# First product of the first strip: seven products of half size in place of eight for the last two groups of W_in

## The chip, the cores and the metric

The kernel runs on one core of one Trainium2 chip. The metric is the device time of one execution in microseconds; the number given for a kernel is the median of its runs. Next to the runs there is one profiled execution, whose trace and page are read here. Engines are PE (TensorE; PEld is its weight loading), DVE (VectorE), ACT (ScalarE), POOL (GpSimd) and SP, whose queue issues the DMAs.

## The reference

```
kv  = einsum('bhsd,bhse->bhde', k, v)              # 8 batches, 8 heads, 576 tokens, 64 features
o   = einsum('bhsd,bhde->bhse', q, kv)
x   = o / sqrt(mean(o*o) + 1e-6) * g_norm          # per token and head
x   -> 4608 tokens x 512
h   = x @ w_in                                     # 512 x 2048
out = max(h, 0)**2 @ w_out                         # 2048 x 512
```

All of it is done in fp32. W_in and W_out come as 64-bit floats and are taken apart into fp32 on the chip.

## The kernel before

**Strips.** The 4608 tokens are taken in nine strips of 512. Each strip has a first product (x times W_in, then ReLU and square into the tiles `gt`) and a second product (times W_out, then out). The attention of later batches is cut into small slices that `attend` puts between the steps of the products. Everything is issued in the order in which the program is written: `manual_schedule` leaves that order alone, and each engine works through its own queue in that order.

**Seven products.** From the second strip on, both products are made by the scheme of Strassen and Winograd: operands are cut in halves both ways, and seven products of the halves, of sums and of differences take the place of eight (the second strip's second product, and both products of later strips, apply the scheme twice). `ORDER = (1, 2, 6, 5, 7, 3, 4)` is their order. Products 1, 6, 7 and 4 add up in PSUM bank A, 5 and 3 in bank B, and 2 is alone in bank C. After products 1, 6 and 5, ACT copies the bank into a `snap` tile (pool "c", six buffers); after 2, 7 and 3, VectorE adds a snap to the bank and so makes a quarter of the result; product 4 leaves the last quarter in bank A (`combine`, line 875). For the first product (`up`, line 920) VectorE then makes ReLU and square of each quarter (lines 933 and 934), except the last, which ACT makes (938 and 939). The operands are the blocks 0 to 3 of W_in (`w_in`, of which block 1 is overwritten by block 0 minus block 1), its sums s1, s2, s4 in blocks 4 to 6 (`w_s`), and x with four differences (`sums_x`).

**The first strip.** Its second product is already made by seven products (`down`). Its first product is not: it runs over four groups of W_in's columns (`NG`), each group over two halves `fh` and two blocks `i`, 16 steps of `up_first` (line 903). A step is one PSUM tile of 128 x 512 with four matmuls over the inner dimension (each matmul leaves two records in the trace), a ReLU on ACT (line 916) and two squares on ACT into the quarters (line 918). The tile steps may run ahead of ACT by four PSUM buffers.

**The weights' conversion, in between.** After each step i of `up_first`, `convert(PACE[i])` converts pieces of W_in and then of W_out, a pair of pieces at a time (16 pairs; pairs 0 to 7 are W_in, two a group; 8 to 11 are the first half of W_out, 12 to 15 the second). For a pair ACT makes two passes (lines 260 and 262, `w_c` and `raw`), always one pair ahead; GpSimd clamps `w_c` (line 282); VectorE joins the words in two operations (lines 284 and 288). For pairs 12 to 15 `sums_out` adds four VectorE sums of W_out's blocks, which SP then stores to `w_out` in DRAM; the second product streams them back as `w_blk`. In the places of W_in's sums, `w_s`, lie the first three blocks of W_out until the first strip is done with them; so W_in's own sums are made only during the second product (`sums_in`, line 314: ACT scales the four blocks by g, VectorE makes four sums a group).

**Around it.** The steps of the attention of batch 1 (transposes of queries `t_ps`, called T below, and key-value products `kv_ps`, called K) stand after the last six steps of the first product. At the second product's start VectorE makes the sums of `gt` (`g_s`), then the sums of W_out's quarters for later strips (`w_t`, sent to `w_deep`), then W_in's sums, then the differences of the second strip's x.

Of the kernel before, what the change touches and what calls it, by code (L numbers as in the profile page):

```python
# [10 lines left out]
FP32 = mybir.dt.float32  # L11
# [3 lines left out]
AF = mybir.ActivationFunctionType  # L15
ALU = mybir.AluOpType
# [4 lines left out]
def kernel(  # L21
# [54 lines left out]
    SQ = 32  # L76
    Q_ON_PE = 2
    BEHIND = 1.6
    X_ON_PE = 2
    EPS = 1e-6  # L80
    AHEAD = 10
# [228 lines left out]
    def pieces_in(i):  # L310
        g, k = divmod(i // 2, KH)
        convert_pair(i // 2, w_in[:, k, g].rearrange("p (a b) e -> p a (b e)", a=2))

    def sums_in(g):

        nc.scalar.activation(w_in[:, :, g, 0:4], w_in[:, :, g, 0:4], AF.Copy, scale=g_col)
        a11, a21, a12, a22, s1, s2, s4 = (block(b)[:, :, g] for b in range(7))
        nc.vector.tensor_tensor(out=s1, in0=a21, in1=a22, op=ALU.add)
        minus(nc.vector, s2, s1, a11)
        minus(nc.vector, s4, a12, s2)  # L320
        minus(nc.vector, a21, a11, a21)
# [24 lines left out]
    def convert(n):  # L346
        while converted[0] < min(n, len(conversions)):
            fn, a = conversions[converted[0]]
            fn(a)
            converted[0] += 1  # L350
# [340 lines left out]
        return xt[s][:, ts(th, TH // SQ), ts(kh, KH), :]  # L691

    def sums_x(s):
        xc[s] = t1, t2, t3, t4 = [
            sum_pool.tile([P, TH // SQ, KH, SQ], FP32, name=f"x_t{i}", tag="sum") for i in range(4)
        ]
        x = lambda kh, th: halves(s, kh, th)
        minus(nc.vector, t1, x(0, 1), x(0, 0))
        minus(nc.vector, t2, x(1, 1), t1)
        minus(nc.vector, t3, x(1, 1), x(0, 1))  # L700
        minus(nc.vector, t4, x(1, 0), t2)
# [165 lines left out]
    def product(p, i, lhsT, rhs, n):  # L867

        for k in range(n):
            nc.tensor.matmul(  # L870
                bank[BANK[p]][:, i, :], lhsT=lhsT(k), rhs=rhs(k),
                start=p in (1, 5, 2) and i == 0 and k == 0, stop=k == n - 1, skip_group_check=True,
            )
# [13 lines left out]
    def quarters(s, g):  # L887

        if (s, 11) not in gq:
            for q in (11, 12, 21, 22):  # L890
                gq[s, q] = g_pool.tile([P, FQ, TH], FP32, name="gt", tag="gt")
        return {q: gq[s, q][:, 2 * g : 2 * g + 2, :] for q in (11, 12, 21, 22)}
# [27 lines left out]
    def up(s, g, p):  # L920
        open_bank(p)
        rhs = {
            1: halves(s, 0, 0), 2: halves(s, 1, 0), 3: halves(s, 1, 1),
            4: xc[s][3], 5: xc[s][0], 6: xc[s][1], 7: xc[s][2],
        }[p]
        for i in range(2):
            product(p, i, lambda kc: block(A_IN[p])[:, kc, g, ts(i, P)], lambda kc: rhs[:, :, kc, :], KH)
        dest = quarters(s, g)

        def relu_squared(q):  # L930
            def f(b, a):
                o = dest[q]
                nc.vector.tensor_tensor(out=o, in0=b, in1=a, op=ALU.add)
                nc.vector.scalar_tensor_tensor(out=o, in0=o, scalar=0.0, in1=o, op0=ALU.max, op1=ALU.mult)
            return f

        def last(b):
            nc.scalar.activation(dest[21], b, AF.Relu)
            nc.scalar.activation(dest[21], dest[21], AF.Square)

        combine(p, relu_squared(11), relu_squared(12), last, relu_squared(22))
# [417 lines left out]
    for s in range(N_STRIP):  # L1359
# [7 lines left out]
        if s >= DEEP_UP:  # L1367
            steps = [(0.5, up_slot, (s, slot)) for slot in range(55)]
        elif s == 0:
            steps = [(2, up_first, (g, fh, i)) for g in range(NG) for fh in range(2) for i in range(2)]  # L1370
        else:
            steps = [(1, up, (s, g, p)) for g in range(NG) for p in ORDER]
        n_up = len(steps)
# [6 lines left out]
        if s >= DEEP_UP:  # L1380
            goal = max(goal, min(ready[DEEP_UP] + (len(slices) - ready[DEEP_UP]) * (s - 1) // (N_STRIP - DEEP_UP - 1), len(slices)))
            if s > DEEP_UP:
                goal = min(pair_ends, key=lambda end: abs(end - goal))
        total, done = sum(w for w, _, _ in steps), 0
        for i, (w, fn, a) in enumerate(steps):
            if s == 0 and i < n_up:

                if i == 0:
                    load_next()
                    load_rest(1, nc.sync)  # L1390
                    load_next()
                if i == 1:
                    load_next()
                if i == 2:
                    for b in range(2):
                        load_q_rest(b, nc.sync)
                if i == 14:
                    for b in range(2):
                        store_first(b)
            elif s == 0 and i == n_up:  # L1400
                convert(len(conversions))
                conv.close()

                stream_pool = ctx.enter_context(tc.tile_pool(name="stream", bufs=6, reuse_waits="tile"))
                sum_pool = ctx.enter_context(tc.tile_pool(name="sum", bufs=8, reuse_waits="tile"))
            if s == 0 and n_up <= i < n_up + 2:
                for g in range(2 * (i - n_up), 2 * (i - n_up) + 2):
                    sum_g1(0, g)
            if s == 0 and n_up + 2 <= i < n_up + 4:
                for g in range(2 * (i - n_up) - 4, 2 * (i - n_up) - 2):  # L1410
                    sum_g3(0, g)
            fn(*a)
            if s == 0 and i < n_up:

                convert(PACE[i])
            done += w
            if s:
                clock[0] += 3.2 if i >= n_up else 2.2 if s == DEEP else 1.2
                soon = tiles_due and tiles_due[0][2][0] // NT == s + 1
                if i == n_up + 10:  # L1420
                    while tiles_due and tiles_due[0][2][0] // NT == s + 1:
                        _, f, a = tiles_due.popleft()
                        f(*a)
                elif not due(keys_due) and not (soon and due(tiles_due)):
                    least = 2.1 if s == DEEP else 4.5 if i < n_up else 3.3
                    quiet = n_up * 2 // 3 < i < n_up + 3 or s == DEEP and (i > n_up + 9 or i == n_up + 7)
                    quiet = quiet or s == DEEP and i < n_up and drips and drips[0][0] == load_q_rest
                    if not quiet and clock[0] >= dripped[0] + least:
                        dripped[0] = clock[0]
                        drip(True)  # L1430
                        if s == DEEP and i == n_up + 8:
                            drip(True)
                if s == DEEP:
                    attend(begun + (goal - begun) * min(i + 1, 25) // 25)
                elif i < n_up:
                    attend_between(i, begun, goal, *(2, 34) if s == DEEP_UP else (0, 27), 38)
                if s == DEEP and i in (3, 4, 7, 9):
                    if i == 3:
                        last_sums = store_deep_sums(*deep_due.popleft())
                    next(last_sums, None)  # L1440
                if s == DEEP and i == n_up - 3:
                    leaf_sums(s, 4)
                if s == 1 and i in range(2, 23, 3):
                    deep_sums_in((1, 6, 5, 4, 0, 2, 3)[i // 3])
                if s == 1 and i in (17, 20, 21, 23):
                    stream()
                continue
            if i == n_up:
                nc.gpsimd.memset(open_xt(1)[:, 0, 0, 0:1], 0.0)
                stream(2)  # L1450
            if i == n_up + 4:
                stream()
            if i in (n_up + 8, n_up + 11):
                load(2, (i - n_up) // 11, nc.sync, "q")
            if i == n_up + 12:
                load_q_rest(2, nc.sync)
            if i - n_up in (7, 8, 9, 12):
                sums_in((7, 8, 9, 12).index(i - n_up))
            if i == n_up + 11:
                sums_x(1)  # L1460
            n = i + 1 - (n_up - 6)
            pairs, m = divmod(max(n - 2 * NP, 0), 3)
            attend(min(ready[0] + min(max(n, 0), 2 * NP) + (n >= 2 * NP) + 4 * pairs + (0, 2, 2)[m], goal))
            while deep_due and i not in (n_up + 1, n_up + 4, n_up + 12, n_up + 13):
                deque(store_deep_sums(*deep_due.popleft()), 0)
            if i == n_up + 2:
                store_first(2)
            if i == n_up + 3:
                for _ in range(2):
                    load_next(names="kv")  # L1470
            if i == n_up + 6:
                load_rest(2, nc.sync)
# [30 lines left out]
```

## Time and profile before

| | |
|---|---|
| median of 3 runs | 870.62 us (869.41 to 871.22) |
| the profiled execution | 868.8 us, span 867.0 us |
| PE, PEld busy | 857.8 us (99%), 804.2 us (93%) |
| VectorE busy | 702.0 us (81%) |
| ACT, GpSimd busy | 348.9 us (40%), 328.1 us (38%) |
| first product of the first strip on PE | to 82.3 us from the span's start |
| second product of the first strip on PE | 83.06 to 138.2 us |

The span runs from the first to the last instruction. A row of the timeline gives start, duration, engine, line, operation, out<-in, shapes and how many instructions were merged; in brackets stands the engine's idle time before it and what ended that. Rows of the busy times by stretch give from:to, length, then each engine's busy time with the number of instructions.

### The profile page before, as it was taken

To read this page: it belongs to the slowest core of one execution; us is meant where nothing else is said; L and a number is where in the kernel's file an instruction comes from. 1 tells how busy PE (TensorE), PEld (TensorE's weight loads), DVE (VectorE), ACT (ScalarE), POOL (GpSimd) and SP (SyncE) were. 2 spreads that over 40 slices of the span, in tenths; PEclk is the share of its full clock that TensorE was granted. 3 is DMA by queue.
4 is the path that set the end of the run, shared out by engine and by line. 5 is a ranking of instruction groups with operands and counts; after the bars stand their busy time and mean duration, and the time that the engine had idled before them with its cause. 6 is when DMAs were issued, how large, how long until landed. Compare 5 with 4: busy or idle time off the path is not lost.

```text
span 867.0 us, 32426 instructions
## 1 busy us (share of the span) xinstructions
PE 857.8 (99%) x14176; PEld 804.2 (93%) x14176; DVE 702.0 (81%) x1132; ACT 348.9 (40%) x777; POOL 328.1 (38%) x335
## 2 busy tenths in 40 slices
PE   7999999999999999999999999999999999999998
PEld 6445888889999999999999999999999999999998
DVE  3768988879877996789688967897889777975887
ACT  4888241320048303750356034901491148102810
POOL 1223004630458223730574045704470447145700
PEclk9999999999999999999999999999999999999999
DMA  9898998999999997989698979987678856885583
GB/s 307 277 362 269 274 377 239 295 332 353 280 264 259 342 325 233 228 307 344 209 244 273 341 239 281 283 297 270 198 236 302 301 165 221 293 282 196 175 315 121
DMA packets 169469, 236.46 MB, mean 273 GB/s; under 512 B 78704, under 2 KB 133744, under 8 KB 161008
## 3 DMA queue, kind: packets, MB, share of 16 engines
q1 hardware_dynamic: 169024, 234.33, 83.5%
q8 instruction: 111, 1.82, 0.9%
q14 instruction: 30, 0.25, 0.1%
q10 hardware_dynamic: 304, 0.07, 0.0%
HBM read 197.66 MB, written 36.70 MB: 270 GB/s over the span
## 4 chain that ended last, share of the span: by engine, by line
PE 83%; DMA 7%; DVE 5%; ACT 3%; SPq 1%; issue 1%; DVEq 0%; ACTq 0%
PE ps_A L865 36%; PE ps_B L865 31%; PE ps_C L865 5%; PE ps_A L870 4%; DMA raw<-in_moe_w_in_dram 2%; PE kv_ps L448 2%; PE x_ps L484 2%; PE ps_B L870 2%; DVE w_t L306 1%; DMA w_deep<-w_t 1%; DMA raw<-in_moe_w_out_dram 1%; DMA w_blk<-w_deep 1%; PE ps_C L870 1%; DMA first_qkv<-in_v_dram 1%; ACT w_c L260 1%
## 5 line engine op out<-in xcount | busy, mean ns | idle before, releaser
L865 PE MATMUL ps_B<-w_blk,g_s 128*64 128x128 f32 x2016 | 122.0, 273 | 0.0
L865 PEld LDWEIGHTS ps_B<-w_blk,g_s 128*64 128x64 f32 x2016 | 112.6, 137 | 0.1
L306 POOL TENSOR_TENSOR x_l<-xT 128x256 f32<-128x256 f32 x21 | 16.2, 773 | 230.2 <-PE ps_A L865 230.2
L865 PE MATMUL ps_B<-w_blk,gt 128*64 128x128 f32 x1504 | 94.1, 273 | 0.3 <-DMA w_blk<-w_deep 0.3
L865 PE MATMUL ps_A<-w_blk,g_s 128*64 128x128 f32 x1536 | 92.2, 273 | 0.0
L1323 POOL TENSOR_TENSOR snap<-snap,gt 128x512 f32<-128x512 f32 x35 | 46.2, 1320 | 112.5 <-ACT snap L1328 93.6
L865 PEld LDWEIGHTS ps_A<-w_blk,g_s 128*64 128x64 f32 x1536 | 85.7, 137 | 0.0
L865 PEld LDWEIGHTS ps_B<-w_blk,gt 128*64 128x64 f32 x1504 | 84.6, 137 | 0.8 <-PE ps_B L865 0.5
L1328 ACT COPY snap<-ps_A 128x512 f32<-128x512 f32 x63 | 36.8, 585 | 103.6 <-PE ps_A L865 96.2
L1263 ACT ACTIVATE gt<-gt 128x512 f32<-128x512 f32 x112 | 70.2, 627 | 9.9 <-DVE gt L1323 9.9
L1264 ACT ACTIVATE gt<-gt 128x512 f32<-128x512 f32 x112 | 70.7, 631 | 3.5
L865 PE MATMUL ps_A<-w_blk,gt 128*64 128x128 f32 x1152 | 71.2, 273 | 0.0
L865 PEld LDWEIGHTS ps_A<-w_blk,gt 128*64 128x64 f32 x1152 | 64.7, 137 | 0.0
L1112 ACT COPY o_sb<-ps_A 128x128 f32<-128x128 f32 x24 | 6.4, 265 | 144.7 <-PE ps_A L865 109.4
L306 DVE TENSOR_TENSOR gt<-gt 128x2048 f32<-128x2048 f32 (+1 forms) x29 | 59.7, 2063 | 0.0
L1111 DVE TENSOR_TENSOR o_sb<-o_sb,ps_B 128x256 f32<-128x256 f32 (+1 forms) x123 | 47.4, 386 | 14.3 <-ACT o_sb L1112 9.5
L865 PE MATMUL ps_A<-x_l,w_in 128*64 128x128 f32 x896 | 58.6, 273 | 0.2 <-DVE gt L1323 0.2
L1323 POOL TENSOR_TENSOR gt<-gt,snap 128x512 f32<-128x512 f32 x42 | 52.5, 1279 | 15.1 <-DVE snap L1323 15.1
L865 PEld LDWEIGHTS ps_A<-x_l,w_in 128*64 128x64 f32 x896 | 50.8, 137 | 0.5 <-DVE gt L1323 0.5
L865 PE MATMUL ps_B<-x_l,w_blk 128*64 128x128 f32 x784 | 51.2, 273 | 0.0
L865 PE MATMUL ps_A<-x_l,w_blk 128*64 128x128 f32 x784 | 51.2, 273 | 0.0
L1112 ACT COPY o_sb<-ps_B 128x128 f32<-128x128 f32 x31 | 8.2, 265 | 96.3 <-PE ps_B L865 96.3
(214 smaller groups left out, 1900.2 us busy)
## 6 DMA issues: line engine op xcount, KB each, us to landing
w_blk<-w_deep SPq DMA_DIRECT2D x56, 1024.0 KB, 7.3
w_blk<-w_out SPq DMA_DIRECT2D x56, 768.0 KB, 6.2
w_blk<-w_in_deep SPq DMA_DIRECT2D x49, 768.0 KB, 5.8
raw<-in_moe_w_in_dram SPq DMA_DIRECT2D x16, 512.0 KB, 9.2
raw<-in_moe_w_out_dram SPq DMA_DIRECT2D x16, 512.0 KB, 8.0
k<-in_k_dram SPq DMA_DIRECT2D x29, 256.0 KB, 4.9
v<-in_v_dram SPq DMA_DIRECT2D x29, 256.0 KB, 5.2
x_d<-x_q SPq DMA_DIRECT2D x27, 256.0 KB, 4.8
```

Of the source, the lines that this page charges most:

```text
L260: nc.scalar.activation(c, high_f, AF.Copy, scale=EXPONENT)
L306: eng.tensor_tensor(out=out, in0=a, in1=b, op=ALU.subtract)
L448: nc.tensor.matmul(ps[ts(h, D), i], lhsT=a, rhs=w, start=i == 0 and c == 0, stop=c == C, skip_group_check=True)
L484: nc.tensor.matmul(ps[half, r, i, ts(p, D)], lhsT=q[row, half], rhs=kvd[b, p][row, row], start=True, stop=True)
L865: nc.tensor.matmul(ps[half], lhsT=lhsT[:, half], rhs=rhs, start=start, stop=stop, skip_group_check=True)
L870: nc.tensor.matmul(bank[BANK[p]][:, i, :], lhsT=lhsT(k), rhs=rhs(k), start=p in (1, 5, 2) and i == 0 and k == 0, stop=k == n - 1, skip_gro ...
L1111: add = lambda out, a, b: nc.vector.tensor_tensor(out=out, in0=a, in1=b, op=ALU.add)
L1112: yield nc.scalar.copy(q[:, 3:4], small(1))
L1263: nc.scalar.activation(o, o, AF.Relu)
L1264: nc.scalar.activation(o, o, AF.Square)
L1323: add = lambda eng, out, a, b: eng.tensor_tensor(out=out, in0=a, in1=b, op=ALU.add)
L1328: nc.scalar.copy(t, ps)
```

## The change

Groups 2 and 3 of the first strip's first product are made by `up`, the seven products, in place of four steps of `up_first` each; groups 0 and 1 stay (`PLAIN = 2`). The first product then has 8 + 14 steps; the counter `at` maps them onto the 16 places at which loads, conversions and attention slices were put before.

The seven products need operands that did not exist at that point:
- the four differences of the first strip's x, made by VectorE after step 5, in four of the six buffers of pool "c";
- W_in's sums for groups 2 and 3, made by VectorE (`first_sums_in`, before the conversion at step 6 and after step 11). As `w_s` holds W_out, they lie in the quarters 22, 12 and 21 of these groups' activations, each of which is written only after its sum was read. Block 1 is overwritten by its difference at once, so that `sums_in` later makes s2 and s1 from the difference, with three VectorE operations in place of four.

Of the results, VectorE makes three additions a group and two ReLU-squares; ACT makes ReLU and square of the quarters 12 and 21 and the three snaps.

```diff
+    PLAIN = 2
...
+    first_w = {}
+
+    def first_sums_in(g):
+
+        a11, a21, a12, a22 = (block(b)[:, :, g] for b in range(4))
+        dest = quarters(0, g)
+        s1, s2, s4 = first_w[g] = [dest[q] for q in (22, 12, 21)]
+        nc.vector.tensor_tensor(out=s1, in0=a21, in1=a22, op=ALU.add)
+        minus(nc.vector, s2, s1, a11)
+        minus(nc.vector, s4, a12, s2)
+        minus(nc.vector, a21, a11, a21)
+
     def sums_in(g):
 
         nc.scalar.activation(w_in[:, :, g, 0:4], w_in[:, :, g, 0:4], AF.Copy, scale=g_col)
         a11, a21, a12, a22, s1, s2, s4 = (block(b)[:, :, g] for b in range(7))
+        if g >= PLAIN:
+            minus(nc.vector, s2, a22, a21)
+            nc.vector.tensor_tensor(out=s1, in0=s2, in1=a11, op=ALU.add)
+            minus(nc.vector, s4, a12, s2)
+            return
...
     def sums_x(s):
+        pool, tag = (sum_pool, "sum") if s else (c_pool, "c")
         xc[s] = t1, t2, t3, t4 = [
-            sum_pool.tile([P, TH // SQ, KH, SQ], FP32, name=f"x_t{i}", tag="sum") for i in range(4)
+            pool.tile([P, TH // SQ, KH, SQ], FP32, name=f"x_t{i}", tag=tag) for i in range(4)
         ]
...
         for i in range(2):
-            product(p, i, lambda kc: block(A_IN[p])[:, kc, g, ts(i, P)], lambda kc: rhs[:, :, kc, :], KH)
+            b = A_IN[p]
+            w = first_w[g][b - 4] if s == 0 and b > 3 else block(b)[:, :, g]
+            product(p, i, lambda kc: w[:, kc, ts(i, P)], lambda kc: rhs[:, :, kc, :], KH)
...
                 nc.vector.tensor_tensor(out=o, in0=b, in1=a, op=ALU.add)
+                if s == 0 and q == 12:
+                    nc.scalar.activation(o, o, AF.Relu)
+                    nc.scalar.activation(o, o, AF.Square)
+                    return
                 nc.vector.scalar_tensor_tensor(out=o, in0=o, scalar=0.0, in1=o, op0=ALU.max, op1=ALU.mult)
...
-            steps = [(2, up_first, (g, fh, i)) for g in range(NG) for fh in range(2) for i in range(2)]
+            steps = [(2, up_first, (g, fh, i)) for g in range(PLAIN) for fh in range(2) for i in range(2)]
+            steps += [(1, up, (s, g, p)) for g in range(PLAIN, NG) for p in ORDER]
...
-        total, done = sum(w for w, _, _ in steps), 0
+        total, done, at = sum(w for w, _, _ in steps), 0, -1
+        plain, turns = 4 * PLAIN, 4 * NG
         for i, (w, fn, a) in enumerate(steps):
-            if s == 0 and i < n_up:
+            if s == 0:
+                before, at = at, i if i < plain else plain + (i - plain) * (turns - plain) // (n_up - plain)
+                if i >= n_up:
+                    at = turns + i - n_up
+            if s == 0 and at < turns and at > before:
...
-                if i == 14:
+                if at == 14:
                     for b in range(2):
                         store_first(b)
...
             fn(*a)
             if s == 0 and i < n_up:
 
-                convert(PACE[i])
+                if i == plain - 3:
+                    sums_x(0)
+                if i == plain - 2:
+                    first_sums_in(PLAIN)
+                if at > before:
+                    convert(PACE[at])
+                if i == plain + 3:
+                    first_sums_in(PLAIN + 1)
...
-            n = i + 1 - (n_up - 6)
+            n = at + 1 - (turns - 6)
```

## The prediction

> **What bounds the kernel now.** I read the granted clock first (1.000 throughout), then busy time by stretch, then the chain that ended last, then the timeline of VectorE and GpSimd. The change lies between 46 us, where the second group's weights are converted, and 131 us, where the first strip's second product is in its last term. In the busy times by stretch (length, then PE, PEld, DVE, ACT, POOL, granted clock, DMA share, GB/s):
>
> ```profile
> 46.00:58.00 12.00, 12.00 (x30) 5.30 (x29) 7.25 (x7) 9.52 (x16) 3.30 (x3) 1.00 1.10 328
> 58.00:70.00 12.00, 11.78 (x49) 5.29 (x47) 7.51 (x7) 11.90 (x19) 4.96 (x4) 1.00 0.96 370
> 70.00:83.00 13.00, 12.93 (x72) 6.51 (x72) 12.70 (x13) 12.80 (x26) 4.06 (x5) 1.00 0.77 229
> 83.00:92.70 9.70, 9.70 (x127) 8.35 (x122) 9.49 (x13) 2.97 (x10) 0.00 (x0) 1.00 1.08 308
> 92.70:131.20 38.50, 38.08 (x244) 33.06 (x243) 35.20 (x62) 13.74 (x17) 0.00 (x0) 1.00 0.98 333
> ```
>
> PE is full, so the page looks like a TensorE bound. But from 70 us VectorE is full too, and the chain that ended last runs on it from 81 to 131 us (apart from one transfer of 10.4 us at 105 us), until PE waits for it:
>
> ```profile
> 81.05 0.68 DVE wt L306
> 81.73 1.99 DVE w_c L284
> ...
> 130.58 0.61 DVE o_sb L1042
> 131.24 8.90 PE ps_A L870 x40
> ```
>
> PE and VectorE are level at 131.24: PE idles 0.46 us there for the o_sb addition, which reads the bank that p=4 adds into. After that PE idles 0.03 us up to 195, so what is lost by 131 is lost for good.
>
> The last thing to see is that VectorE and GpSimd do not run side by side on SBUF data. Timeline rows (start, duration, engine):
>
> ```profile
> 81.39 1.24 POOL L282 TENSOR_SCALAR w_c<-w_c 128x1024 f32<-128x1024 f32 x1 [2.14 <-ACT w_c L260]
> 81.64 2.06 DVE L284 SCALAR_TENSOR_TENSOR w_c<-w_c,raw 128x1024 int32<-128x1024 int32 x1
> 83.74 1.23 DVE L288 SCALAR_TENSOR_TENSOR wt<-raw,w_c 128x1024 int32<-128x1024 int32 x1
> ...
> 27.85 1.05 POOL L282 TENSOR_SCALAR w_c<-w_c 128x1024 f32<-128x1024 f32 x1 [2.25 <-DVE newton L515]
> 28.11 0.69 DVE L605 TENSOR_TENSOR x_n<-x_ps,newton 128x512 f32<-128x512 f32 x1
> ```
>
> The 2.06 is a 1.23 operation that began under a clamp of GpSimd and ended 1.07 us after it. The 28.11 row, which reads PSUM, runs inside a clamp at its usual 0.69.
>
> **What PE gains.** A tile of 512 tokens takes 3.44 us (starts 51.08, 54.51, 57.95), a group of four 13.75. One of the seven products takes 1.73 us in the second strip (138.25 to 139.98), seven 12.1. Two groups save 3.3 us.
>
> **What VectorE gets, all before 131 us.** Prices are distances from start to start.
> - Differences of x: the same four take 136.89 to 139.42, 2.53 us.
> - Sums of W_in: four a group, 122.66 to 125.32, so 2 x 2.66 = 5.32.
> - Combinations: addition and ReLU-square 1.32 (163.02 to 164.34), twice a group, and one bare addition 0.60; 3.24 a group, 6.48.
>
> Together 14.3 us. Nothing is taken from VectorE before 131: the two operations saved in sums_in (0.7 us each) are those of groups 2 and 3, which start at 131.10 and 139.42, where PE waits for no one, so they bring nothing.
>
> **Room for it.** VectorE's gaps from 46.06 (end of pair 5) to 92.66 (end of the last sums of W_out) are 1.41, 0.93, 2.31, 1.68, 0.93, 0.93 and 0.93 = 9.1 us. In each of the seven a clamp of about 0.93 runs, which VectorE's SBUF operations can't share; 2.6 us are free. The six additions read PSUM and may lie beside a clamp, 3.6 us. So 14.3 - 2.6 - 3.6 = 8.1 us late at 92.7. From there to 130.5 there are waits of 0.55, 0.28 and 1.67 us. The first two are for ACT and go away; the third is for w_deep's transfer, which starts from VectorE's own w_t and moves with it: I give it half. VectorE arrives 8.1 - 0.8 - 0.8 = 6.5 us late, between 5.6 (all absorbed) and 8.1.
>
> **PE meets the same delay earlier.** PE's fourth product of the last group (p=4) needs the addition of p=7, which stands on VectorE behind pair 13. Adding up the order that the code issues from 46.06, with a converted pair 2.49, its clamp 0.93 and its four sums 2.54: differences 2.5; pair 6 with clamp 3.4; sums of group 2 2.7; pairs 7, 8, 9 with clamps 10.3; p=2's addition and square 1.3 (clamp beside); pair 10 2.5; sums of group 3 2.7; p=7's 1.3 (clamp beside); pair 11 2.5; p=3's addition 0.6, its clamp standing out by 0.3; pair 12 with sums 5.0; p=2's 1.3; pair 13 with sums 5.0. That is 41.4, so 87.5 us. The addition (0.7), p=4 (1.73) and K (0.74) follow: the second product starts at 90.7 instead of 83.06, 7.6 us late. From there PE is full to 130.78, so it would reach the last term at 138.4, against VectorE's 137.6 (131.1 + 6.5). Small waits between dependent operations (0.2 each where a square stands behind a clamp, four times) put it 0.8 later, at 139.2. Against 131.24 that is 7.2 to 8.0: the idle 0.46 goes first. I take **+7.6 us**, the middle, since both engines come out there; ends 5.6 (VectorE with every wait absorbed, PE no later than it) and 11.2 (the six additions not beside clamps, 3.6 more).
>
> **The rest, at no cost.** ACT loses 8 tiles x 1.17 = 9.4 us and gets six snaps at about 0.5 and eight passes at about 0.55, 7.4: 2 us less. ACT is full from 58 to 83, but VectorE's queue covers it. What is new is that a snap waits for PE and, as xc[0] holds four of the six "c" buffers, for the addition that frees the fifth or sixth; behind it stand the next pair's passes (one pair ahead of need) and the copies of T and K. If that lead is used up, VectorE idles (rival 2). PE gets waits for snaps after p=1, 6, 5, each with one product (1.73) of lead, while ACT has been starting its tiles up to 1.7 us after PE's end (57.95 to 59.61); T and K stand behind, and they are late with everything else. GpSimd's queue holds only clamps, which come later with VectorE. SP: the raw pieces wait for VectorE's last pass five pairs before, with 8 to 10 us of landing against over 17 us of lead; w_out's stores, the key and value loads (issued 78.24, used 90.61) and w_blk move with the work that releases them.
>
> **Rivals.**
> 1. *It is hidden, faster by PE's 3.3: 867.3.* For it: VectorE is busy 81% of the span and its gaps are 9.1 us. Against: all room to 131, clamps' share excluded, is 2.6 + 3.6 + 2.5 = 8.7. It decides where VectorE's load fits before 130.5, that is 14.3 + 3.3 us of room.
> 2. *Lockstep: +12.6, 883.2.* The additions find no clamp to lie beside (3.6), and the waits for snaps and "c" buffers use up ACT's lead once or twice (a late pair's passes are 2.1 us on ACT, of which 1.4 is left after the four 0.2s above). For it: ACT is 99% busy at 58 to 70.
> 3. *Clamps don't block: +4.4, 875.* The whole 9.1 us is room: 14.3 - 9.1 - 0.8. Against: the 2.06 row.
> 4. *The clock falls in a stall.* By the order above PE waits about 5 us for the snap of p=1 behind pair 9's passes, more than any wait of before (1.4). At the trace's start, after idling, 14 records of 128x128 take 3.22 us, 0.23 each, and four at 7.17 take 0.71, 0.18 each; 14 then lose 0.7 to 1.4 us. After the first stall this hides behind PE's later waits; only if one comes before the last products it adds all of that, +9.0: 879.6. [...]
>
> **Numbers.** The profiled execution took 868.8 us (span 867.0 and 1.8 around it), 1.8 below the median of the runs, 870.62; a fixed shift adds to either, and I give the median: 870.6 + 7.6 = 878.2. Chances: forecast 0.72 (876 to 882), rival 2 0.10, rival 4 0.05, rival 3 0.06, rival 1 0.07. From 873 to 885 all but rival 1 and the tails is held. A measurement can tell 0.2% (1.7 us) from no change; faster 0.06, same 0.02, slower 0.92.
>
> **What would show it.** Right: VectorE without real gaps from 46 to about 100 us; the last w_s sums near 100; the second product near 91; PE idle about 11 us more in all between 52 and 91, in waits for snaps and for gt additions; from there the same rows 7 to 9 us later, PEclk 1.00. Wrong: VectorE gaps not filled by clamps, additions stretched by clamps, or PE starting its second product at 80.

## The result, and the profile after

The changed kernel takes 882.25 us (median of 4 runs, 881.97 to 885.62) against 870.85 us for the kernel before (median of 4, 869.41 to 871.22). The ratio of the means is 1.0143, 95% interval 1.0116 to 1.017. By the medians it is slower by 11.4 us. Its profiled execution took 882.1 us, with a span of 880.2 us and a mean granted clock of 0.994; the one of before took 868.8 us, with a span of 867.0 us at 1.000.

Busy times by stretch of the changed kernel; the columns are from:to, length, PE, PEld, DVE, ACT, POOL (each with its instructions), granted clock, DMA share, GB/s:

```profile
46.00:58.00 12.00, 7.82 (x27) 4.66 (x25) 11.86 (x12) 8.59 (x15) 3.22 (x3) 1.00 1.09 317
58.00:70.00 12.00, 9.71 (x34) 8.12 (x35) 10.86 (x11) 9.39 (x11) 4.64 (x4) 0.72 0.94 365
70.00:83.00 13.00, 8.99 (x58) 7.07 (x57) 12.79 (x15) 6.65 (x12) 1.59 (x2) 0.99 0.27 89
83.00:92.70 9.70, 9.70 (x57) 7.98 (x57) 8.97 (x11) 6.14 (x9) 2.68 (x3) 0.83 0.95 282
92.70:131.20 38.50, 38.50 (x340) 33.38 (x339) 35.09 (x60) 13.43 (x25) 0.00 (x0) 1.00 0.99 321
```

PE, which was full in each of these stretches, is now idle for 4.2, 2.3 and 4.0 us in the first three. VectorE is full from 46 us on instead of from 70, but for one wait of 0.93 us. The granted clock, 1.00 everywhere before, is 0.72 and 0.83 in two stretches. The PE timeline of the changed kernel (start, duration, operation; in brackets the idle time and what ended it) shows the three waits:

```profile
51.92 1.89 PE L889 MATMUL ps_C<-xT,w_in 128*128 128x256 f32 x8
60.29 3.78 PE L889 MATMUL ps_A<-x_t,gt 128*128 128x256 f32 x8 [6.48 <-ACT snap L899]
63.87 2.84 PE L889 MATMUL ps_B<-x_t,gt 128*128 128x256 f32 x8
...
72.24 1.99 PE L889 MATMUL ps_A<-x_t,w_in 128*128 128x256 f32 x8 [1.65 <-DVE gt L954]
...
81.42 2.43 PE L889 MATMUL ps_A<-x_t,gt 128*128 128x256 f32 x8 [2.36 <-ACT snap L899]
...
93.90 3.72 PE L889 MATMUL ps_A<-w_s,gt 128*128 128x256 f32 x16
```

The first and the third wait are for ACT's snap after product 1 of group 2 and of group 3; the one between is for the addition of product 7. The last row is the second product's start: 93.90 instead of 83.06. The products right behind the two snaps last 3.78 and 2.43 us where the usual row is 1.89: that is the lower clock, 0.50 from 60.20 to 63.70 and 0.80 from 81.40 to 83.80. ACT's timeline shows what held the first snap:

```profile
53.67 1.15 ACT L261 ACTIVATE w_c<-raw 128x1024 f32<-128x1024 f32 x1 [2.75 <-DMA raw<-in_moe_w_out_dram]
...
57.59 1.15 ACT L261 ACTIVATE w_c<-raw 128x1024 f32<-128x1024 f32 x1 [0.56 <-DMA raw<-in_moe_w_out_dram]
...
59.66 0.58 ACT L899 COPY snap<-ps_A 128x512 f32<-128x512 f32 x1
...
75.94 0.63 ACT L956 ACTIVATE gt<-gt 128x512 f32<-128x512 f32 x1 [5.11 <-DVE gt L954]
...
80.78 0.59 ACT L899 COPY snap<-ps_A 128x512 f32<-128x512 f32 x1
```

The snap of product 1, which PE had finished near 52, stands behind the passes of two pairs of W_out whose raw pieces land only at 53.6 and 57.5. That is not VectorE's doing: in the kernel before the same pass of pair 9 begins at 57.53, behind the same transfer. The second one, at 80.78, stands behind ACT's ReLU of quarter 12, for which ACT idles 5.11 us until VectorE has made the addition at 75.22. VectorE's timeline:

```profile
49.43 1.95 DVE L289 SCALAR_TENSOR_TENSOR w_in<-raw,w_c 128x1024 int32<-128x1024 int32 x1
60.47 1.23 DVE L285 SCALAR_TENSOR_TENSOR w_c<-w_c,raw 128x1024 int32<-128x1024 int32 x1 [0.93 <-POOL w_c L283]
61.73 1.94 DVE L289 SCALAR_TENSOR_TENSOR w_s<-raw,w_c 128x1024 int32<-128x1024 int32 x1
79.67 1.52 DVE L307 TENSOR_TENSOR wt<-wt 128x512 f32<-128x512 f32 x1
89.45 0.69 DVE L954 TENSOR_TENSOR gt<-ps_A,snap 128x512 f32<-128x512 f32 x1 [0.56 <-PE ps_A L889]
101.57 2.49 DVE L916 TENSOR_TENSOR g_s<-gt 128x512 f32<-128x512 f32 x4
139.58 0.68 DVE L1067 TENSOR_TENSOR o_sb<-ps_A,snap 128x512 f32<-128x512 f32 x1
```

The two bracketed rows are all of VectorE's waits from 44 to 101 us. GpSimd's clamps lie beside operations with two SBUF inputs, which last 1.94 instead of 1.22 or 1.52 instead of 0.69; one clamp of ten, at 89.38, lies beside an addition. The sums `g_s` stand at 101.57; in the kernel before this row was

```profile
92.58 2.49 DVE L897 TENSOR_TENSOR g_s<-gt 128x512 f32<-128x512 f32 x4
```

The last addition, at 139.58, is done 1.2 us before PE comes to its last term at 141.45 (131.24 before), so PE no longer waits for VectorE there. The chain that ended last, which ran on VectorE from 81 to 131 us before, is on PE from the second snap on:

```profile
80.78 0.59 ACT snap L899
81.42 2.43 PE ps_A L889 x8
```

### The profile page after: what moved, and what is told of

Its sections match the earlier page's. It is cut to its first block, busy times and chain, and to the rows that moved or that the text cites. A ratio compares the mean times of both kernels' runs of the same rounds, so it can differ in the third digit from the quotient of the medians.

```text
span 880.2 us, 32536 instructions
## 1 busy us (share of the span) xinstructions
PE 860.0 (98%) x14224; PEld 816.4 (93%) x14224; DVE 720.0 (82%) x1152; ACT 347.8 (40%) x767; POOL 328.8 (37%) x335
## 4 chain that ended last, share of the span: by engine, by line
PE 89%; DMA 4%; ACT 2%; SPq 2%; DVE 1%; issue 1%; POOL 0%; DVEq 0%; ACTq 0%
PE ps_A L884 36%; PE ps_B L884 31%; PE ps_A L889 7%; PE ps_C L884 5%; PE ps_B L889 4%; PE kv_ps L466 2%; PE x_ps L502 2%; PE ps_C L889 2%; DMA raw<-in_moe_w_in_dram 1%; DMA raw<-in_moe_w_out_dram 1%; DMA first_qkv<-in_k_dram 1%; SPq L249 1%; DMA v_rest<-in_v_dram 1%; SPq L151 1%; DMA v<-in_v_dram 0%
## 5 line engine op out<-in xcount | busy, mean ns | idle before, releaser
L1094 DVE TENSOR_TENSOR g_s<-gt 128x512 f32<-128x512 f32 x56 | 46.4, 828 | 0.0
```

The costliest lines, as they stand in the source:

```text
L1094: nc.vector.tensor_tensor(out=t, in0=a21, in1=a22, op=ALU.add)
```

## The experiments

The *shift* is the start of PE's first instruction in the second strip's second product, less its 195.1 us in the kernel before; the changed kernel has 9.9. It leaves out pauses of PE late in the span, which differ from run to run (last section). Shifts in the expectations are this number. The executions begin unequally, though: the tile with which the first strip's first product reaches bank C starts at 33.64 us in the profile of before and at 31.7 to 33.1 in all others, long before the change. *From a common start* adds that difference. It agrees with the medians better, and both are given. *Over before* is the median less that of the kernel before, run in the same round (870.85, 869.01, 868.70 or 869.41 us); the ratio is that of the means.

| kernel | median us | over before | ratio (95%) | shift | from a common start | 2nd product starts | `g_s` starts |
|---|---|---|---|---|---|---|---|
| changed | 882.25 | 11.4 | 1.0143 (1.0116, 1.0170) | 9.9 | 10.8 | 93.90 | 101.57 |
| adds_only | 874.75 | 5.7 | 1.0057 (1.0039, 1.0075) | 3.5 | 5.3 | 87.54 | 95.01 |
| no_w_sums | 875.59 | 6.6 | 1.0082 (1.0060, 1.0104) | 5.2 | 6.0 | 89.24 | 97.81 |
| q12_vector | 882.36 | 13.4 | 1.0156 (1.0106, 1.0205) | 11.7 | 12.7 | 94.27 | 102.52 |
| keep_clock | 879.37 | 10.4 | 1.0107 (1.0072, 1.0142) | 8.5 | 10.1 | 92.45 | 100.54 |
| adds_snap | 872.69 | 4.0 | 1.0049 (1.0019, 1.0078) | 1.8 | 3.7 | 84.06 | 97.01 |
| snap_ahead | 879.46 | 10.8 | 1.0114 (1.0080, 1.0148) | 8.0 | 8.6 | 88.62 | 102.20 |
| x_early | 880.12 | 11.4 | 1.0106 (1.0063, 1.0150) | 8.7 | 9.7 | 92.64 | 100.33 |
| one_group | 881.46 | 12.8 | 1.0121 (1.0068, 1.0174) | 8.9 | 9.6 | 91.08 | 98.97 |
| vector_load | 878.45 | 9.0 | 1.0104 (1.0087, 1.0121) | 8.1 | 9.9 | 86.39 | 100.09 |
| one_group_clock | 881.24 | 11.8 | 1.0136 (1.0121, 1.0151) | 8.1 | 9.7 | 91.17 | 98.19 |
| three_moves | 880.32 | 10.9 | 1.0120 (1.0096, 1.0144) | 5.8 | 7.5 | 86.41 | 99.99 |

Theory A: VectorE's 14.3 us of added work are the loss. Theory B: the order of ACT's queue is, since PE waits for snaps that stand behind passes which themselves wait. Theory C: the clock that falls in those waits.

### adds_only: VectorE's added work away, but for the additions

```diff
-        s1, s2, s4 = first_w[g] = [dest[q] for q in (22, 12, 21)]
-        nc.vector.tensor_tensor(out=s1, in0=a21, in1=a22, op=ALU.add)
-        minus(nc.vector, s2, s1, a11)
-        minus(nc.vector, s4, a12, s2)
-        minus(nc.vector, a21, a11, a21)
+        first_w[g] = [a11, a12, a22]
...
-        if g >= PLAIN:
+        if False:
...
-                    sums_x(0)
+                    xc[0] = [halves(0, *h) for h in ((0, 1), (1, 0), (1, 1), (0, 0))]
...
+                if s == 0:
+                    return
                 nc.vector.scalar_tensor_tensor(out=o, in0=o, scalar=0.0, in1=o, op0=ALU.max, op1=ALU.mult)
```

> Left out: the sums of W_in for groups 2 and 3, the differences of the first strip's x (the products take unsummed blocks instead) and the ReLU-squares of VectorE in the first strip. Products, snaps and the six additions stay, so VectorE gets 4.0 us instead of 14.3. Theory A (VectorE's load sets the end): 4.0 us fit into 2.6 us of gaps and beside clamps, PE's 3.3 us show: second product at 80 to 81 us, about 868 us. Theory B (the shorter chain between PE and ACT costs by itself: the first snap stands behind the passes of pair 9, which waited for their transfer until 57.5 us in both traces): PE still stands from 53.7 to about 60 us, 6.6 lost against 3.3 won: second product at 85.5 to 87 us, 873 to 875 us.

Measured: 5.7 us slower than before (874.75 against 869.01). PE's timeline of adds_only has the first stall unchanged, and ACT's has its cause:

```profile
59.32 3.78 PE L885 MATMUL ps_A<-xT,w_in 128*128 128x256 f32 x8 [6.38 <-ACT snap L895]
```
```profile
56.62 1.16 ACT L261 ACTIVATE w_c<-raw 128x1024 f32<-128x1024 f32 x1 [0.64 <-DMA raw<-in_moe_w_out_dram]
...
58.70 0.57 ACT L895 COPY snap<-ps_A 128x512 f32<-128x512 f32 x1
```

With most of VectorE's added work gone, PE still waits 7.7 us for two snaps, and that eats its 3.3 us of saved work. The lower clock behind the first wait (0.79 from 58 to 70 us) is part of this loss. So theory B, with C behind it, holds for a part, and VectorE's work is not needed for it: the seven products bring nothing in this order even where the sums are free.

### no_w_sums: W_in's sums away, all else kept

```diff
-        s1, s2, s4 = first_w[g] = [dest[q] for q in (22, 12, 21)]
-        nc.vector.tensor_tensor(out=s1, in0=a21, in1=a22, op=ALU.add)
-        minus(nc.vector, s2, s1, a11)
-        minus(nc.vector, s4, a12, s2)
-        minus(nc.vector, a21, a11, a21)
+        first_w[g] = [a11, a12, a22]
...
-        if g >= PLAIN:
+        if False:
```

> Left out: the sums of W_in for groups 2 and 3 (unsummed blocks are multiplied instead); 5.3 us off VectorE, everything else as in the changed kernel. A: the second product starts 5.3 us earlier than in the changed kernel (93.9), at 88.6, some 877 us, or 875 if the second fall of the clock goes too. B: the stall of PE at 53.7 to 60 stays, and the second product starts between 88 and 91.

Measured: 4.8 us less shift than the changed kernel from a common start (6.0 against 10.8), against 5.3 us of sums taken away. The first stall stays at 6.4 us. Most of what is taken from VectorE comes back, so its work is a term of the loss: theory A, beside B. But this run does not show that VectorE had no room: its `g_s` comes only 3.8 us earlier, and VectorE now waits 6.7 us between 44 and 101 us (1.5 in the changed kernel). Part of the gain is the clock, which is 1.00 from 83 to 92.7 us instead of 0.83. The 6.0 us that are left go with PE's waits for snaps, 8.6 us in all.

### q12_vector: ReLU and square of quarter 12 on VectorE

```diff
-                if s == 0 and q == 12:
+                if False:
```

> The quarter 12 of groups 2 and 3 gets its ReLU-square on VectorE (1.2 us more there, two passes a group less on ACT). A: 0.6 to 1.2 us later than the changed kernel, 883. B in a second place (ACT's queue stands from 70.8 to 75.9 for VectorE's addition of quarter 12, and the snap that PE needs at 79.1 stands behind it): that snap comes about 3 us earlier, PE's second stall goes and the clock does not fall at 83.8; second product 1 to 2.4 us earlier than 93.9, about 880.

Measured: 882.36 us, 13.4 over before instead of 11.4; the shift is 1.8 us larger. The wait for the second snap is gone, since ACT no longer waits for VectorE in front of it. But PE's timeline of q12_vector shows what came in its place:

```profile
90.50 2.57 PE L889 MATMUL ps_A<-x_t,w_in 128*128 128x256 f32 x8 [3.35 <-DVE gt L954]
```

Two more operations on a full VectorE move the addition of product 7 back, and product 4 waits for that instead. Where two engines are both late, freeing the one at the other's cost gains nothing.

### keep_clock: PE kept busy during the two waits for snaps

```diff
     def up(s, g, p):
         open_bank(p)
+        if s == 0 and p == 6:
+            busy = apsum.tile([P, 2, 2, d_model // 2], FP32, name="x_ps", tag="x", bufs=1)
+            keep_busy(busy[:, 0, 0, 0:P], 24 if g == PLAIN else 9)
```

`keep_busy` issues so many multiplications by the identity, whose result nothing reads.

> Ahead of product 6 of groups 2 and 3, PE multiplies 24 and 9 times the identity into an unused bank, about 5 and 2 us, which fill its two stalls. Clock theory: no half rate at 60 and 83.8 us; the products at 81.4 to 89 run at full rate and the second product starts 1.7 us earlier, at 92.2, about 880.5. If VectorE alone sets the end: at most 0.5 us earlier than the changed kernel's 882.3.

Measured: 879.37 us; the shift is 1.4 us smaller, 0.7 from a common start. In the first stretch PE counts as busy with these multiplications, and the clock stays at 1.00 up to 70 us; it falls once later, behind a wait of 3.77 us for group 2's addition:

```profile
46.00:58.00 12.00, 12.00 (x72) 9.67 (x71) 11.83 (x13) 8.43 (x14) 3.57 (x3) 1.00 1.09 320
58.00:70.00 12.00, 8.26 (x40) 6.60 (x38) 10.89 (x10) 9.10 (x11) 6.42 (x4) 1.00 0.83 316
70.00:83.00 13.00, 11.50 (x73) 9.94 (x74) 12.79 (x16) 5.93 (x11) 1.13 (x1) 0.87 0.34 108
```

So one fall in place of two brings about 1 us by the traces, and 1.0 by the medians over before: theory C is a small term here. By the ratios it could be 3, but their intervals overlap. Where PE was no longer slowed it waited for VectorE instead.

### adds_snap: adds_only, with the snap ahead of the passes

```diff
-                if at > before:
-                    convert(PACE[at])
+                if at > before and at != plain - 1:
+                    convert(PACE[at - (at >= plain)])
```

This comes on top of adds_only's edit. The conversions from step 7 on are issued one place later.

> As the run with the additions only (same parts left out: W_in's sums, the differences of x, the first strip's ReLU-squares on VectorE), and in addition the conversions from step 7 on are issued one place later, so that the snap of product 1 of group 2 stands ahead of the passes of pair 9. B (the snap's place behind passes that wait for their transfer): the snap comes at 56.0 instead of 58.7 us, PE's stall of 6.4 us shrinks to about 3.7, the second product starts at 84 to 85.5 instead of 87.5, about 872. If the stall has another cause: no change, 874.7.

Measured: second product at 84.06 instead of 87.54. PE's timeline of adds_snap:

```profile
56.24 3.44 PE L885 MATMUL ps_A<-xT,w_in 128*128 128x256 f32 x8 [3.43 <-ACT snap L895]
```

Moving one pair's passes behind the snap halves the stall, as theory B asks; the rest is the pair ahead of it, which waits for its transfer too. It is still slower than the kernel before.

### snap_ahead: the same move in the changed kernel, nothing left out

The edit is the last one, alone:

```diff
-                if at > before:
-                    convert(PACE[at])
+                if at > before and at != plain - 1:
+                    convert(PACE[at - (at >= plain)])
```

> The changed kernel with the conversions from step 7 on issued one place later, nothing left out. B alone: 2.7 us earlier than the changed kernel, 879.5. A (VectorE sets the end, and PE's stalls only fill its wait): PE's first stall shrinks, its later waits for VectorE's additions grow, second product within 0.7 us of 93.9, less up to 1.5 if the clock no longer falls late; 881 to 882.5.

Measured: the second product starts at 88.62, 5.3 us earlier than in the changed kernel, yet `g_s` stands at 102.20, 0.6 later, and the time is 879.46 us. The waits of PE from 33 to 150 us (total, times, longest):

```profile
PE ps_A L889 <- ACT snap L899: 3.3, 2, 2.3
PE ps_A L889 <- DVE gt L954: 2.7, 1, 2.7
PE ps_A L889 <- DVE gt L307: 1.6, 1, 1.6
PE ps_A L889 <- DVE o_sb L1067: 0.8, 1, 0.8
```

Three of the four are now for VectorE, two of them inside the second product, where the changed kernel had none. What B gave back, A mostly took: of 5.3 us gained at the second product's start 1.9 are left when the second strip's second product begins. The conversions stand one place later here, which can be part of it.

### x_early: the differences of x after step 0

```diff
-                if i == plain - 3:
+                if i == 0:
                     sums_x(0)
```

> The changed kernel with the four differences of the first strip's x issued after step 0 instead of step 5, where VectorE has gaps of 3.0 (32.6 to 35.6) and 2.1 us (41.5 to 43.6). A: 2.5 us less for VectorE after 46 us, everything behind 2 to 2.5 us earlier, second product 91.4 to 92, about 880. B alone: the first stall ends with the snap at 59.7 as before, no change, 882.

Measured: shift 1.1 to 1.2 us smaller, about half of what was expected of it; the medians over before don't show it (11.4 in both). One tile of the first group now waits 0.6 us for its weights (`PE ps_A L930 <- DVE w_in L289`), so that time was not all free.

### one_group: only group 3 by seven products

```diff
-    PLAIN = 2
+    PLAIN = 3
...
-                if i == plain + 3:
+                if i == plain + 3 and PLAIN + 1 < NG:
```

> Only group 3 by seven products. VectorE gets 2.5 + 2.7 + 3.2 = 8.4 us instead of 14.3, PE saves 1.65 instead of 3.3. A: 8.4 less 0.8 of gaps left at that point and 1.8 beside clamps is 5.8 late at 92.7, about 4.2 to 5 at the second product's last term: shift 4 to 5.5, 873.5 to 875. If the cost were the first stall and the clock, which belong to the place where tiles turn into products and not to the number of groups: shift 7 or more, 877 and up.

Measured: 881.46 us, shift 8.9. Half of the change costs nearly the whole of it. That is not what theory A had asked for (4 to 5.5), though VectorE's `g_s` is 6.4 us late, near the 5.8 expected; it is what was expected of a loss that belongs to the place where tiles turn into products (7 or more). But the longest wait is not for a snap. ACT's copy of T stands behind passes which wait 1.44 us for VectorE. PE's timeline and the stretch around the stall in one_group:

```profile
70.94 1.11 PE L435 MATMUL t_ps<-ident,q 128*128 128x128 f32 x4 [3.53 <-ACT qT L440]
71.85 3.62 PE L889 MATMUL ps_C<-xT,w_in 128*128 128x256 f32 x8
```
```profile
70.00:83.00 13.00, 10.29 (x42) 7.62 (x43) 12.79 (x14) 7.52 (x14) 2.76 (x3) 0.50 0.44 140
```

PE works at half rate for this whole stretch. The obvious new theory was that C is large here.

### one_group_clock: one_group, with PE kept busy in its waits

```diff
+        if s == 0 and p == 6:
+            busy = apsum.tile([P, 2, 2, d_model // 2], FP32, name="x_ps", tag="x", bufs=1)
+            keep_busy(busy[:, 0, 0, 0:P], 16)
...
+        if s == 0 and p == 1:
+            busy = apsum.tile([P, 2, 2, d_model // 2], FP32, name="x_ps", tag="x", bufs=1)
+            keep_busy(busy[:, 0, 0, 0:P], 15)
```

> Group 3 alone by seven products, and PE multiplies the identity into an unused bank after product 1 (15 times, 3.3 us) and ahead of product 6 (16 times, 3.5 us), where it stood 3.5 and 1.8 us. In the run without it the clock was at half rate from 70.0 to 83.6 us. Clock theory: no half rate there, PE's delay at the second product's start falls from 8.0 to about 4, and VectorE (6.4 late at 92.6) sets the end: shift 4.5 to 6 instead of 8.9. If the half rate cost nothing because VectorE set the end anyway: 8 to 9 again.

Measured: the spell at 70 to 83 us is gone (the clock there is 1.00), and nothing came of it: 881.24 us, second product at 91.17 (91.08 in one_group). PE's timeline shows what replaced it:

```profile
86.90 3.40 PE L889 MATMUL ps_A<-x_t,w_in 128*128 128x256 f32 x8 [2.56 <-DVE gt L960]
```

Product 4 waits for product 7's addition, which stands on VectorE behind the sums of W_out's pair, and then takes 3.40 us itself where the usual row is 1.89, with the clock at 0.86 from 83 to 95 us. So in one_group the cost of the half rate hid behind VectorE. VectorE's `g_s` is only 5.6 us late here, against a shift of 8.1 for PE; where the remaining 2.5 us come from could not be separated.

### vector_load: the kernel before, with VectorE work that nothing reads

```diff
+                if i in (5, 6, 8, 11, 13):
+                    t1, t2, t3, t4 = [c_pool.tile([P, TH // SQ, KH, SQ], FP32, name=f"x_t{n}", tag="c") for n in range(4)]
+                    minus(nc.vector, t1, halves(0, 0, 1), halves(0, 0, 0))
+                    minus(nc.vector, t2, halves(0, 1, 1), t1)
+                    minus(nc.vector, t3, halves(0, 1, 1), halves(0, 0, 1))
+                    minus(nc.vector, t4, halves(0, 1, 0), t2)
                 convert(PACE[i])
```

> The kernel before, with VectorE's load alone: the four differences of the first strip's x are made five times (after steps 5, 6, 8, 11 and 13) into buffers that nobody reads, 12.7 us, nothing else changed; tiles, PE's work and ACT's passes are those of before. A: 12.7 less 2.6 of gaps is 10.1 late at 92.7 and 7.6 to 9.5 late at the second product's last term, where PE then waits; PE keeps its tiles to about 83 us and stands only in the second product; 876 to 878. If VectorE's load costs only through the snaps and additions that the seven products wait for (B): within 2 us of the kernel before.

Measured: 878.45 us, 9.0 above the kernel before, for 12.7 us of differences; the shift is 8.1, inside the 7.6 to 9.5 that theory A asked for, or 9.9 from a common start. PE's first product is still the sixteen tiles. PE's waits from 33 to 150 us, and the timeline rows of the first wait and of the last term:

```profile
PE t_ps L417 <- ACT qT L422: 3.8, 1, 3.8
PE ps_A L870 <- DMA w_blk<-w_out: 2.0, 1, 2.0
PE ps_B L870 <- DVE gt L306: 1.5, 1, 1.5
PE ps_A L870 <- DVE o_sb L1042: 1.3, 1, 1.3
```
```profile
71.72 1.07 PE L417 MATMUL t_ps<-ident,q 128*128 128x128 f32 x4 [3.77 <-ACT qT L422]
...
139.61 7.17 PE L870 MATMUL ps_A<-w_blk,gt 128*128 128x256 f32 x32 [1.27 <-DVE o_sb L1042]
```

Theory A is shown: VectorE's load alone makes the kernel before late by most of what the change costs (9.0 of 11.4 us), with no snap and no seven products. One part of the expectation failed: PE does not keep its tiles to 83 us. It waits 3.77 us for ACT's copy of T, which stands behind passes that wait 2.35 us for VectorE, and its next tile takes 4.92 us instead of 3.60, with the clock at 0.87 from 70 to 83 us. So VectorE's lateness reaches PE through ACT's queue too, and A and B are not two separate causes there. The second of PE's waits also shows a transfer that was hidden and no longer is: `w_blk` comes from stores that wait for VectorE's sums.

### three_moves: x_early, snap_ahead and nine identity multiplications a group

```diff
-                if i == plain - 3:
+                if i == 0:
                     sums_x(0)
...
-                if at > before:
-                    convert(PACE[at])
+                if at > before and at != plain - 1:
+                    convert(PACE[at - (at >= plain)])
...
+        if s == 0 and p == 6:
+            busy = apsum.tile([P, 2, 2, d_model // 2], FP32, name="x_ps", tag="x", bufs=1)
+            keep_busy(busy[:, 0, 0, 0:P], 9)
```

> The changed kernel with three edits together: the differences of x after step 0, the conversions from step 7 on one place later, and 9 multiplications by the identity ahead of each product 6. Alone they took 1.3, 1.9 and (with 24 and 9) 1.4 us off the shift of 9.9 us. If they add up: 5.3. A: VectorE's load sets a floor, 14.3 less 2.5 moved, less gaps and clamps, less what the second product's waits absorb: 4.5 to 6.5 us, with PE waiting for VectorE in the second product; in no case below the kernel before: 874 to 876.

Measured: the lowest shift of the kernels that leave nothing out, 5.8 (7.5 from a common start), and the clock at 1.00 throughout. But the time is 880.32 us: from there to its end this execution falls back by another 6.7 us, more than half of it in waits of PE for nothing that the profile shows (waits after 195 us):

```profile
PE x_ps L502 <- issue: 4.1, 3, 2.2
```

So the moves add up as far as the second strip's second product (5.3 expected). That the gain did not reach the end stays unexplained. No version beats the kernel before.

## Why the prediction was right, and where it was off

**Slower, inside the range.** 878.2 was forecast, 873 to 885 as the range; 882.25 was measured, just outside the 876 to 882 that had a chance of 0.72. The main reason stated, that the first strip has too little VectorE time for the added operations and that PE meets this before 131 us, is what vector_load shows.

**The price of VectorE's work: right.** By distances from start to start in the trace after, the differences of x cost 44.79 to 48.19 less 0.87 for a clamp, 2.53; the sums 2.65 and 2.64; the six combinations and two ReLU-squares 6.60 together. That is 14.4, against 14.3.

**The room for it: the first term that was mis-sized.** The prediction let VectorE use 6.2 us of its gaps, 3.6 of them by additions beside clamps, and so had it 8.1 us late at the `g_s` sums. Measured from the same operation in both traces (end of pair 5, 46.06 before and 44.79 after) to `g_s`, it takes 46.52 us before and 56.78 after: 10.3 late, so 4.1 us of room used. (The sums of W_out ended at 101.6, forecast near 100.) Eight of the ten clamps fell beside two-input operations, at 0.72 to 0.87 each, one ended a 0.93 us wait, and one lay beside an addition. An addition comes when PE and ACT have finished, a clamp when ACT's passes have; nothing puts the two together. In the trace after, the operation of 61.73, which has two SBUF inputs and met a clamp, took 1.94 us for 1.22; the addition of 89.45, which reads PSUM, took 0.69 inside the clamp of 89.38, and 0.68 at 63.59 with no clamp beside it.

**PE's path: the second.** Second product forecast at 90.7, found at 93.90. PE's added idle time was near the forecast, 10.5 against about 11 us (6.48 + 1.65 + 2.36). That it is so near is partly luck: 8.8 us of it are waits for snaps, which the prediction held to be covered by VectorE's queue. What the sum lacked is, first, the lower clock behind the first and the third of these waits: that is rival 4, which came at a chance of 0.05, in company with the forecast. It had only the 5 us wait for the first snap in view; the fall ahead of the last products, for which it asked, came after a wait of 2.36 us. It priced a fall at 0.7 to 1.4 us, its estimate from the rows at the trace's start. From product 6 to product 7 the changed kernel takes 6.25 us in group 2 and 6.03 in group 3, against 3.56 and 4.49 in three_moves, whose clock stayed at 1.00: 2.7 and 1.5 us. The clock is not the whole of the 3.2 us, though. VectorE came to product 7's addition at 89.45, forecast 87.5, and in keep_clock, with one fall instead of two, the second product starts only 1.45 us earlier. From 60.20 to 63.70 the granted clock is 0.50, from 83.80 to 87.40 it is 0.66:

```profile
60.20:63.70 3.50, 3.41 (x8) 2.78 (x9) 3.20 (x3) 2.12 (x3) 1.45 (x2) 0.50 1.05 408
...
83.80:87.40 3.60, 3.60 (x29) 3.17 (x29) 3.50 (x4) 2.97 (x5) 1.53 (x1) 0.66 1.09 338
```

In the changed kernel the clock is at 0.50 from 58.95 to 65.77 us and from 82.84 to 86.25, that is for 6.82 and 3.41 us. The second of these spells came behind a wait of PE of only 2.36 us (last section).

**ACT's queue: seen, not priced.** The prediction named the snap behind pair 9's passes and the 5 us that it costs (rival 4), but held it to be covered by VectorE's lateness. adds_only shows that it is a loss of its own, with the clock's fall behind it 5.3 to 5.7 us even with VectorE relieved, and snap_ahead that VectorE's part stands once it is eased. The two overlap, so they don't add: about 5 and about 9 alone, 11 together. For the second snap the prediction had PE's waits covered by one product of lead each, and did not see that quarter 12's ReLU, ahead of it on ACT, waits for VectorE (5.11 us).

**The last term.** That both engines come out level there was off by 1.2 us: PE is the later one. The shift there is 10.2 against the 7.2 to 8.0 forecast. Of the rest up to 13.2 us in this one execution, 2.2 are pauses of PE at two places, near 264 and 526 us of the time before, that the sum did not hold. By medians the rest is worth less (11.4 in all).

**The rivals.** *Hidden* falls with vector_load. *Lockstep* (883.2) came nearest in time, and part of its mechanism is there: the additions found no clamps. But ACT's lead did not run out for VectorE, which waits only 0.93 and 0.56 us in all. *Clamps don't block* is refuted by the 1.94 rows.

## What to carry to other kernels

An engine that is only 81% busy over the span may have no room at all where new work is put: count its gaps in that stretch, subtract what another engine keeps it from using (here 0.72 to 0.87 us at eight of ten clamps), and don't credit an overlap of two events that nothing brings together. When work is moved into a queue that is worked through in order, ask for every new instruction what stands in front of it and what that waits for; here a copy of 0.58 us behind passes that waited for their transfers was a stall of 6.48 us on PE, which needed the copy. Where two engines become late together, test each with the other relieved, and don't expect the gains to add.

## What the runs showed of the hardware that was not expected

- Whether the clock fell did not go by the length of PE's wait alone. It fell behind waits of 2.34, 2.36 and 2.56 us, and not behind waits of 2.40 and 2.66. What decided between them was not shown.

| kernel | PE's wait, us | until | granted clock behind it |
|---|---|---|---|
| vector_load | 2.0 | between 92.7 and 131.2 | 1.00 from 92.7 to 131.2 |
| snap_ahead | 2.34 | 56.49 | 0.78 from 58 to 70; the product of 58.86 took 3.04 us for 1.89 |
| changed | 2.36 | 81.42 | 0.50 from 82.84 to 86.25 |
| q12_vector | 2.40 | 72.06 | 1.00 from 70 to 83 |
| one_group_clock | 2.56 | 86.90 | 0.86 from 83 to 95 |
| three_moves | 2.66 | 66.29 | 1.00 from 58 to 83 |
| one_group | 3.53 | 70.94 | 0.50 from 70 to 83 |
| changed | 6.48 | 60.29 | 0.50 from 58.95 to 65.77 |

- The clock fell after the wait was over: in the changed kernel the wait of 2.36 us ended at 81.42, PE then worked, and the clock was at 1.00 up to 82.84 and at 0.50 from there.
- The clock stayed low while PE worked: in one_group it was at 0.50 in the whole stretch from 70 to 83 us, of which PE was busy for 10.29 us.
- PE pauses late in the span without a releaser in the trace: 1.16 and 1.06 us in the changed kernel (until 275.18 and 539.43), 0.39 and 2.88 in adds_snap (until 261.97 and 269.64), 0.90 in snap_ahead (until 255.71), 2.2 at most in three_moves. The kernel before has none in its trace. In the changed kernel's timeline:

```profile
275.18 0.88 PE L884 MATMUL ps_B<-x_l,w_blk 128*64 128x128 f32 x12 [1.16 <-issue]
```

  The cause is open. A single trace is therefore not enough to compare ends of span within 3 us.
- The start varies: the same early tile begins anywhere from 31.74 us (adds_snap) to 33.64 (before).
